# One core, attention and MLP block: last 64 rows of Q, K, V in halves of the array, a ninth key/value slot, residual in bf16, first two tiles side by side

## The chip, the cores and the metric

The kernel runs on one core of one Trainium2 chip. The metric is the device time of one execution in microseconds (us). TensorE is called PE here, VectorE DVE, ScalarE ACT, GpSimd POOL and the sync engine's DMA queue SP, as in the profile.

## The reference

`x` is 2048 rows of D = 576. There are 32 heads of 18, each position attends to 8 keys at distances 0, 2, ..., 14, and the MLP is F = 4608 wide.

```python
h  = x + attn(layernorm(x)) @ wo            # q, k, v = layernorm(x) @ wqkv
y  = layernorm(layernorm(h))
h2 = h + gelu(y @ w1 + b1) @ w2 + b2
```

Inputs and output are bf16.

## The kernel before

**Tiles.** Row 16p + j of `x` lies on partition p of tile j, so a tile has 128 rows and there are 16 tiles (n is the place in the order of work, j = `ORDER[n]`: the even tiles from 14 down, then the odd ones). A key at distance 2w is in tile j - 2w of the same partition, or, past the tile's start, in the partition above. Each parity has a window of eight slots (`kwin[e]`, `vwin[e]`). When a slot's tile has been used at its own place, it is wanted by the later tiles shifted by one partition: the kernel writes K and V of the tile to DRAM (`kvd`, task `bw`) and reads them back one row lower into the same slot (`ks`, `vs`), after that tile's product with the window is done.

**Stages per tile.** LayerNorm 1: statistics on DVE (`ln1a`), the root on POOL (`ln1r`), the normalising on DVE for the first eight tiles and on ACT for the rest (`ln1b`). The tile is padded with zeros from 576 to 640 columns and turned into `xnT`, by five PE transposes and an ACT copy for n < 8 (`t1`, `t1e`), by DMA for the rest. K, V and Q are each ten products 128x288 on PE (`chunk`, task `c`: two column halves of five blocks of 128 rows, the last block half zeros), evicted by ACT (`e`). Attention is on DVE: `p1a` (window times q), a tree of additions, `p1b` (maximum over the slots, subtract), exp on ACT, `p2n` (sum and divide), `p2a` (window times weights), additions to `o` (`p2b`). Then `o` is transposed (`t2`), by PE for n < 3 and by DMA after that, multiplied with `wo` (18 products, pairs of 64-row halves of the array), copied to `h` in f32 by ACT (`woe`), and DVE adds `x` and takes the statistics of LayerNorm 2 (`ln2a`); `hb` is `h` + b2 in bf16 for the end; `ln2b` normalises on ACT and `t3` transposes.

**MLP.** Two tiles make a group (eight groups). First come nine units `u`, 36 products each, in 64-row halves of the array, each followed by a gelu on ACT into `hT`. Then come four passes (two tiles times two column halves), each of 36 products 128x288 in nine pieces `m`, which add up in one PSUM bank `po`. After each pass DVE adds `hb` and writes `osb` (`fin`, task `out`), and after two passes the tile is stored. `po` is a pool of two tiles of one bank each; the other PSUM user is a pool `pm` of three tiles of two banks.

**Order.** All tasks are put in order while the kernel is built: `Weaver.run` takes, again and again, the task that can start first by costs written beside it, ties by priority, and records its instructions at once. Every engine then runs its instructions in that order. Waits between engines are put in by the tile framework from which instruction, in the order of recording, last wrote or read a tile.

Of the kernel before, what the change touches and what calls it, by code (L numbers as in the profile page):

```python
# [15 lines left out]
class Weaver:  # L16
# [4 lines left out]
    def __init__(self, slots):  # L21
        self.tasks = {}
        self.slots = {tag: [0.0] * n for tag, n in slots.items()}
        self.held = {}

    def add(self, name, engine, cost, fn, after=(), prio=0.0, take=None, give=(), lag=0.1, table=None, kb=0.0,
            backlog=2.5, transfers=1):
        assert name not in self.tasks, name
        self.tasks[name] = (engine, cost, fn, tuple(after), prio, take, tuple(give), lag, table,
                            (kb, backlog, transfers))  # L30


    RATE, TABLE, LANES = 240.0, 1.28, 8

    def run(self):
# [8 lines left out]
        table, queue, landed = None, 0.0, [0.0] * self.LANES  # L44
        while left:
            best = None
            for n in ready:
                engine, cost, fn, after, prio, take, give, lag, tab, (kb, backlog, transfers) = left[n]
                start = max([clock.get(engine, 0.0)] + [done[a][2 if done[a][0] == engine else 1] for a in after])
                if take is not None:  # L50
                    tag, key = take
                    if key not in self.held:
                        if not self.slots[tag]:
                            continue
                        start = max(start, min(self.slots[tag]))
                if kb:
                    start = max(start, queue - backlog, landed[transfers - self.LANES - 1])
                rank = (round(start, 3), prio, n)
                if best is None or rank < best:
                    best = rank  # L60
            assert best is not None, sorted(left)[:40]
            start, _, n = best
            engine, cost, fn, after, prio, take, give, lag, tab, (kb, backlog, transfers) = left.pop(n)
            ready.discard(n)
            if take is not None and take[1] not in self.held:
                tag, key = take
                free = min(self.slots[tag])
                self.slots[tag].remove(free)
                self.held[key] = tag
            fn()  # L70
            if tab is not None and tab != table:
                cost += self.TABLE
                table = tab
# [8 lines left out]
            for key in give:  # L82
                self.slots[self.held.pop(key)].append(done[n][1])
# [7 lines left out]
def kernel(  # L91
# [37 lines left out]
    dram = ctx.enter_context(tc.tile_pool(name="dram", bufs=1, space=bass.MemoryType.DRAM))  # L129
    ps_po = ctx.enter_context(tc.tile_pool(name="ps_po", bufs=2, space=bass.MemoryType.PSUM))  # L130
    ps_pm = ctx.enter_context(tc.tile_pool(name="ps_pm", bufs=3, space=bass.MemoryType.PSUM))

    kvd = dram.tile([NT, P + 1, 2 * D], BF16, name="kvd")
# [15 lines left out]
    kwin = [wpool.tile([P, W, D], BF16, name=f"kwin{e}") for e in range(2)]  # L149
    vwin = [wpool.tile([P, W, D], BF16, name=f"vwin{e}") for e in range(2)]  # L150
# [16 lines left out]
    HB, HT, LG, NQ = 4, 9, 4, 13  # L167
# [3 lines left out]
    wv = Weaver({"po": 2, "pm": 3, "oT": 1, "h": 2, "xr": 2, "hb": HB,  # L171
# [5 lines left out]


    TP, TO = 8, 3
    SLACK = 0.6  # L180
    WARM = 11
# [9 lines left out]
    def x_load(n):  # L191
        def fn():
            nc.sync.dma_start(out=T["x", n][:, 0:D], in_=x3[:, ORDER[n], :])
# [9 lines left out]
    def wq_rest(eng, t):  # L203
        return lambda: eng.dma_start(out=wqkv_sb[0:64, 4, t * D:(t + 1) * D], in_=A_wqkv[512:576, t * D:(t + 1) * D])
# [30 lines left out]
    Q, K, V = 0, 1, 2  # L235
    for n in range(NT):
        if n < LENT:
            T["x", n] = kwin[1][:].rearrange("p w c -> p (w c)")[:, n * DP:(n + 1) * DP]
        elif n < LENT + XH:
            T["x", n] = hn_bufs[0][:].rearrange("p a b -> p (a b)")[:, (n - LENT) * DP:(n - LENT + 1) * DP]  # L240
        else:
            T["x", n] = early.tile([P, DP], BF16, name=f"x{n}")[:]
        load(f"x{n}", x_load(n), 147, prio=0.1 * n if n else -300)
    for t in (K, V, Q):
        eng, at = (nc.scalar, -200) if t == K else (nc.sync, 0.55 if t == Q else 0.75)
        for r, (part, fn, kb) in enumerate((("a", wq_load(eng, t, 0, 2), 295), ("b", wq_load(eng, t, 2, 4), 295),
                                            ("c", wq_rest(eng, t), 74))):
            add(f"W{t}{part}", "ACT" if t == K else "SP", 0.5, fn, (), at + 0.01 * r, lag=1.8, kb=kb)

    def b2_load():  # L250
        nc.sync.dma_start(out=b2_bc[:], in_=B_b2.partition_broadcast(P))
        nc.sync.dma_start(out=kvd[:, 0, :], in_=w2_sb[0:NT, 0:2, :].rearrange("p a c -> p (a c)"))

    load("b2", b2_load, 150, prio=8.5, issue=0.7, transfers=2)
# [6 lines left out]
    for c in range(W1C):  # L261
        for half in range(2):
            for k in range(0, KC, W1K):
                bulk(f"w1{c}{half}{k}", w1_chunk(c, half, k), 295, prio=20 + c)
    for c in range(W2C):
        bulk(f"w2{c}", w2_chunk(c), 295, prio=30 + c, after=("b2", "b1t", "warm"))
# [5 lines left out]

    for n in range(NT):
        nc.vector.memset(T["x", n][:, D:DP], 0.0)
        if n in (1, 3, 5):
            t = (K, V, Q)[n // 2]
            nc.vector.memset(wqkv_sb[64:128, KT - 1, t * D:(t + 1) * D], 0.0)
    nc.vector.memset(w2_sb[0:NT, 0:2, :], 0.0)


    def warm():
        pw = ps_pm.tile([P, 1024], F32, tag="pm", name="warm")
# [3 lines left out]
    add("warm", "PE", 5.0, warm, (), -400, take=("pm", "warm"), give=("warm",))  # L286

    def b1_turn():
        T["b1T"] = ps_pm.tile([P, 2048], BF16, tag="pm", name="b1T")[:, 0:FT]
# [26 lines left out]
    def transposed(src, shifted=False):  # L316
        starts = [kt * P for kt in range(KT)] + ([64 + kt * P for kt in range(KT - 1)] if shifted else [])
        pt = ps_pm.tile([P, 2048], BF16, tag="pm", name="pt")[:, 0:len(starts) * P]
        pt = pt.rearrange("p (k t) -> p k t", t=P)
        for k, c0 in enumerate(starts):  # L320
            nc.tensor.transpose(pt[:, k, :], src[:, c0:c0 + P], ident[:])
        return pt

    def region(n):
        return n if n < LENT else (0, 1, 2, 3, 0, 1, 0)[n - LENT]


    def front(n):  # L330
# [3 lines left out]
        def ln1a():  # L334
            ln_stats(L1, n, T["x", n][:, 0:D])
            if n >= W:
                ln_var(nc.vector, L1, n, (1.0, EPS))

        def ln1r():
            if n < W:  # L340
# [6 lines left out]
        def ln1b():  # L347
            if n < W:
                nc.vector.tensor_scalar(out=T["x", n][:, 0:D], in0=T["x", n][:, 0:D], scalar1=L1["mv"][:, n, 0:1],
                                        scalar2=L1["rs"][:, n, :], op0=ALU.subtract, op1=ALU.mult)  # L350
            else:
                nc.scalar.activation(out=T["x", n][:, 0:D], in_=T["x", n][:, 0:D], func=ACT.Identity,
                                     scale=L1["rs"][:, n, :], bias=nmr[:, n, :])

        def t1():
            T["pt1", n] = transposed(T["x", n])

        def t1e(by_dma=False):
            if n < 2 * LENT:
                flat = (vwin if n < LENT else kwin)[1][:].rearrange("p w c -> p (w c)")  # L360
                r = region(n)
                T["xnT", n] = flat[:, r * DP:(r + 1) * DP].rearrange("p (k t) -> p k t", k=KT)
            else:
                T["xnT", n] = early.tile([P, KT, P], BF16, name=f"xnT{n}")[:]
            if by_dma:
                nc.sync.dma_start(out=T["xnT", n], in_=T["x", n], transpose=True)
            else:
                nc.scalar.copy(out=T["xnT", n], in_=T["pt1", n])  # L368

        add(f"ln1a{n}", "DVE", 1.07 if n < W else 1.2, ln1a, (f"x{n}",) + (("ln1b0",) if n == 1 else ()), prio=-20 + n if n < W else 0.5 + (n - W) // 4)  # L370
        add(f"ln1r{n}", "POOL", 0.95 if n < W else 1.1, ln1r, (f"ln1a{n}",), prio=-20, lag=0.1 if n < W else 1.0)
        add(f"ln1b{n}", "DVE" if n < W else "ACT", 0.45 if n < W else 0.7, ln1b, (f"ln1r{n}",), prio=-20 + n)
        freed = [m for m in range(LENT, n) if n < 2 * LENT and region(m) == region(n)][-1:]
        room = [f"t1e{m}" for m in range(LENT) if not freed and LENT <= n < 2 * LENT]
        room += [f"c{m}{c}" for m in freed for c in "QKV"]
        if n < TP:
            add(f"t1{n}", "PE", 0.45, t1, [f"ln1b{n}"] + room, prio=-60, take=("pm", f"t1{n}"), lag=0.3)
            add(f"t1e{n}", "ACT", 0.7, t1e, (f"t1{n}",), prio=-150, give=(f"t1{n}",))
        else:
            load(f"t1e{n}", lambda: t1e(True), 164, [f"ln1b{n}"] + room, prio=-20 + n, issue=1.2, lag=3.0)  # L380

        def chunk(t):
            def fn():
                pq = ps_pm.tile([P, 1024], F32, tag="pm", name="pq")
                T["pq", n, t] = pq
                for half in range(2):
                    c0 = t * D + half * HALF
                    p0 = 512 - HALF + half * HALF  # L390
                    for kt in range(KT):
                        nc.tensor.matmul(pq[:, p0:p0 + HALF], lhsT=T["xnT", n][:, kt, :],  # L392
                                         rhs=wqkv_sb[:, kt, c0:c0 + HALF],
                                         start=(kt == 0), stop=(kt == KT - 1))
            return fn

        def evict(t):
            def fn():
# [3 lines left out]
                else:  # L402
                    dst = (kwin if t == K else vwin)[e][:, s, :]
# [329 lines left out]
```

## Time and profile before

| | us |
|---|---|
| median of 3 runs (lowest, highest) | 382.62 (382.17, 382.90) |
| the profiled execution, whole | 382.82 |
| its span, first to last instruction | 381.0 |
| first PE instruction starts, last product's end | 1.17, 377.60 |
| PE busy, share of the span | 373.8, 98% |
| DVE busy, share | 292.5, 77% |
| ACT busy, share | 209.0, 55% |

The granted PE clock is 1.00 throughout. Products overlap, so the mean duration of one (286 ns for 128x288) is not its price: their starts lie 123 ns apart. DMA is busy for about the first 100 us (weights, `x` and the shifts) and lightly after that.

### The profile page before, as it was taken

To read this page: it belongs to the slowest core of one execution; us is meant where nothing else is said; L and a number is where in the kernel's file an instruction comes from. 1 tells how busy PE (TensorE), PEld (TensorE's weight loads), DVE (VectorE), ACT (ScalarE), POOL (GpSimd) and SP (SyncE) were. 2 spreads that over 40 slices of the span, in tenths; PEclk is the share of its full clock that TensorE was granted. 3 is DMA by queue.
4 is the path that set the end of the run, shared out by engine and by line. 5 is a ranking of instruction groups with operands and counts; after the bars stand their busy time and mean duration, and the time that the engine had idled before them with its cause. 6 is when DMAs were issued, how large, how long until landed. Compare 5 with 4: busy or idle time off the path is not lost.

```text
span 381.0 us, 10766 instructions
## 1 busy us (share of the span) xinstructions
PE 373.8 (98%) x4618; PEld 304.8 (80%) x4618; DVE 292.5 (77%) x563; ACT 209.0 (55%) x437; POOL 32.4 (9%) x55
## 2 busy tenths in 40 slices
PE   7999999999999999999999999999999999999996
PEld 3777787788788887887788778877887788778874
DVE  7999999899999999999999899998968932010000
ACT  2896665888255762575257526870685088106700
POOL 3670011000110110010001100110011011000000
PEclk9999999999999999999999999999999999999999
DMA  8798999986523212352232333222313331000000
GB/s 254 229 193 273 211 226 236 308 270 199 99 48 101 69 22 64 50 80 62 48 94 64 49 77 82 48 65 61 80 41 56 93 80 25 11 15 19 2 17 15
DMA packets 63967, 38.48 MB, mean 101 GB/s; under 512 B 39520, under 2 KB 63904, under 8 KB 63920
## 3 DMA queue, kind: packets, MB, share of 16 engines
q1 hardware_dynamic: 63296, 37.13, 41.4%
q8 instruction: 36, 0.59, 0.6%
q10 hardware_dynamic: 624, 0.66, 0.5%
q14 instruction: 11, 0.09, 0.1%
HBM read 22.28 MB, written 6.52 MB: 76 GB/s over the span
## 4 chain that ended last, share of the span: by engine, by line
PE 72%; DVE 14%; DMA 2%; issue 1%; POOL 0%; ACT 0%; DVEq 0%; ACTq 0%
PE po L667 35%; PE pm L630 33%; PE pw L564 4%; DVE prod L444 3%; DVE prod L450 2%; DVE prod L485 2%; DMA kwin<-kvd 2%; DVE prod L491 1%; DVE l_st L306 1%; DVE prod L495 1%; DVE h L577 1%; DVE half L437 0%; DVE half L438 0%; DVE hb L590 0%; DVE lg L457 0%
## 5 line engine op out<-in xcount | busy, mean ns | idle before, releaser
L641 ACT ACTIVATE hT<-pm,b_sb 128x256 bf16<-128x256 f32 x288 | 112.5, 477 | 88.6 <-PE pm L630 88.3
L630 PE MATMUL pm<-hnT,w_sb 64*128 64x256 bf16 x2592 | 144.7, 269 | 0.0
L667 PE MATMUL po<-w_sb,hT 128*128 128x288 bf16 x1152 | 142.9, 286 | 0.0
L630 PEld LDWEIGHTS <-w_sb 64*128 64x128 bf16 x2592 | 125.7, 94 | 17.1 <-issue 1.8
L667 PEld LDWEIGHTS <-hT 128*128 128x128 bf16 x1152 | 111.9, 98 | 29.9 <-issue 2.0
L686 DVE TENSOR_TENSOR osb<-po,hb 128x288 bf16<-128x288 f32 x32 | 14.2, 453 | 56.0 <-PE po L667 56.0
L314 POOL TENSOR_TENSOR l_rs<-l_ve,mhalf 128x1 f32<-128x1 f32 x32 | 27.0, 844 | 277.8 <-DVE l_ve L310 277.2
L450 DVE TENSOR_TENSOR prod<-prod 128x2304 bf16<-128x2304 bf16 (+1 forms) x64 | 44.1, 690 | 1.5
L444 DVE TENSOR_TENSOR prod<-kwin,q 128x4608 bf16<-128x4608 bf16 x16 | 40.9, 2555 | 1.3 <-DMA kwin<-kvd 0.9
L485 DVE TENSOR_TENSOR prod<-vwin,at 128x4608 bf16<-128x4608 bf16 x16 | 40.9, 2554 | 0.5 <-ACT vwin L405 0.2
L594 ACT ACTIVATE hn<-h,nmr,l_rs 128x576 bf16<-128x576 f32 (+1 forms) x32 | 19.2, 652 | 23.1 <-issue 13.3
L392 PE MATMUL pq<-wqkv_sb,vwin 128*128 128x288 bf16 x210 | 27.5, 286 | 1.4 <-ACT vwin L368 0.8
L392 PE MATMUL pq<-wqkv_sb,kwin 128*128 128x288 bf16 x210 | 27.1, 286 | 0.0
L392 PEld LDWEIGHTS <-vwin 128*128 128x128 bf16 x210 | 20.1, 98 | 6.9 <-ACT vwin L368 1.2
L392 PEld LDWEIGHTS <-kwin 128*128 128x128 bf16 x210 | 20.2, 98 | 5.4 <-issue 0.5
L491 DVE TENSOR_TENSOR prod<-prod 128x2304 bf16<-128x2304 bf16 x16 | 21.7, 1358 | 0.6
L564 PE MATMUL pw<-wo_sb,oT 64*128 64x288 bf16 x288 | 20.3, 283 | 0.0
L577 DVE TENSOR_TENSOR h<-h,xr 128x576 f32<-128x576 f32 x16 | 12.0, 753 | 10.4 <-ACT h L569 10.4
L569 ACT COPY h<-pw 128x576 f32<-128x576 f32 x16 | 10.5, 654 | 15.4 <-PE pw L564 15.4
L564 PEld LDWEIGHTS <-oT 64*128 64x128 bf16 x288 | 13.6, 94 | 4.3 <-issue 1.2
L405 ACT CAST vwin<-pq 128x576 bf16<-128x576 f32 x16 | 10.2, 641 | 6.9 <-PE pq L392 6.9
L405 ACT CAST kwin<-pq 128x576 bf16<-128x576 f32 x16 | 10.2, 639 | 6.3 <-PE pq L392 6.3
(63 smaller groups left out, 224.8 us busy)
## 6 DMA issues: line engine op xcount, KB each, us to landing
w_sb<-in_B_w_dram SPq DMA_DIRECT2D x36, 288.0 KB, 5.7
xr<-in_A_x_dram SPq DMA_DIRECT2D x16, 144.0 KB, 2.3
out_dram<-osb SPq DMA_DIRECT2D x16, 144.0 KB, 1.9
kvd<-kwin SPq DMA_DIRECT2D x14, 144.0 KB, 4.4
kvd<-vwin SPq DMA_DIRECT2D x14, 144.0 KB, 4.0
kwin<-kvd SPq DMA_DIRECT2D x14, 144.0 KB, 3.0
vwin<-kvd SPq DMA_DIRECT2D x14, 144.0 KB, 2.1
wqkv_sb<-in_A_wqkv_dram SPq DMA_DIRECT2D x4, 288.0 KB, 5.6
```

The source lines that it names most:

```text
L314: nc.gpsimd.tensor_tensor(out=L["rs"][:, n, :], in0=L["ve"][:, n, :], in1=mhalf[:], op=ALU.pow)
L392: nc.tensor.matmul(pq[:, p0:p0 + HALF], lhsT=T["xnT", n][:, kt, :], rhs=wqkv_sb[:, kt, c0:c0 + HALF], start=(kt == 0), stop=(kt == KT - 1))
L405: nc.scalar.copy(out=dst.rearrange("p (d h) -> p d h", h=H), in_=src.rearrange("p h d -> p d h"))
L444: nc.vector.tensor_tensor(out=prod[:], in0=kwin[e][:], in1=T["q", n][:].unsqueeze(1).to_broadcast([P, W, D]), op=ALU.mult)
L450: nc.vector.tensor_tensor(out=pv[:, :, 0:b - a, :], in0=pv[:, :, 0:b - a, :], in1=pv[:, :, a:b, :], op=ALU.add)
L485: nc.vector.tensor_tensor(out=prod[:].rearrange("p w (d h) -> p w d h", d=Dh, h=H), in0=vwin[e][:].rearrange("p w (d h) -> p w d h", d=Dh, ...
L491: nc.vector.tensor_tensor(out=prod[:, 0:4, :], in0=prod[:, 0:4, :], in1=prod[:, 4:8, :], op=ALU.add)
L564: nc.tensor.matmul(pw[:, half, 0:HALF], lhsT=T["oT", n][lo:lo + 64, block(c, half), :], rhs=wo_sb[lo:lo + 64, c, :], start=(c == 0), stop= ...
L594: nc.scalar.activation(out=hn_slots[n % 2][:, c0:c1], in_=src, func=ACT.Identity, scale=L2["rs"][:, n, :], bias=nmr[:, n, :])
L630: nc.tensor.matmul(pm[:, half, q, 0:width], lhsT=w1_sb[lo:lo + 64, c, f0:f0 + P], rhs=T["hnT", g][lo:lo + 64, block(c, half), 0:width], st ...
L641: nc.scalar.activation(out=T["hT", g, u][:, half, q, 0:width], in_=T["pm", g, u][:, half, q, 0:width], func=ACT.Gelu_apprx_tanh, bias=b1_s ...
L667: nc.tensor.matmul(T["po", n, half][:], lhsT=T["hT", g, u][:, r, q, a * P:(a + 1) * P], rhs=w2_sb[:, ft, half * HALF:(half + 1) * HALF], s ...
```

## The change

1. **Q, K, V.** The last 64 rows of the product are no longer padded. `xnT` and `wqkv_sb` hold these rows twice, on partitions 0 to 63 and 64 to 127; each column half takes its own copy in its own half of the array (`rest`). Eight 128-row products and one pair of 64-row ones take the place of ten. Two chunks that follow each other put their pairs back to back (`table="flip"`). The copies are made by two more 64-column transposes per PE transpose (`transposed`, 64 columns to one half of the PSUM partitions), by the loads `dup` for tiles turned by DMA, and by `wq_rest`. `xnT` now lies in the end of `w2_sb`, so the second half of the w2 chunks is loaded after the tiles' products.
2. **Window.** One tile of 17 slots for both parities; the shift is one SBUF to SBUF transfer of 127 partitions into the next slot, after the tile before. `p1a` and `p2a` skip one slot and are two instructions in most tiles. `kvd` and its transfers are gone.
3. **Softmax.** Three instructions over the slots become one `tensor_reduce`, for the maximum and for the sum.
4. **Residual.** `h` is bf16 and becomes `h` + b2 in place after `ln2b`; `hb` as a tile is gone.
5. **PSUM.** One pool of four tiles of two banks. Until Q, K and V are done the fourth serves transposes and products; from then on it is the tile `pos`, whose two banks are the two `po` of before.
6. **Start.** `x` of the second tile is loaded through the ACT queue at once, half of K's weights through SP; statistics of tile 1 go ahead of the normalising of tile 0, which is done in two pieces, as is its eviction; most clearing on DVE is gone, and one of eleven warming products.
7. The planner knows a price for changing between 64-row and 128-row work on PE, several costs are new, and the group units wait for all Q, K, V products.

```diff
-                for half in range(2):
-                    ...
-                    for kt in range(KT):
-                        nc.tensor.matmul(pq[:, p0:p0 + HALF], lhsT=T["xnT", n][:, kt, :], ...
+            blocks = [(half, kt, 0, P) for half in range(2) for kt in range(KT - 1)]
+            rest = [(half, KT - 1, 64 * half, 64 * half + 64) for half in range(2)]
+            todo = rest + blocks if wv.table["PE"] == "64" else blocks + rest
+            for half, kt, lo, hi in todo:
+                ...
+                nc.tensor.matmul(pq[:, p0:p0 + HALF], lhsT=T["xnT", n][lo:hi, kt, :],
+                                 rhs=wqkv_sb[lo:hi, kt, c0:c0 + HALF], ...
 ...
+    def transposed(key, src, tail, shifted=False):
+        ...
+        for k in range(KT - 1):
+            nc.tensor.transpose(pt[:, k, :], src[:, k * P:(k + 1) * P], ident[:])
+        for lo, c0 in ((0, D - 64), (64, tail)):
+            nc.tensor.transpose(pt[lo:lo + 64, KT - 1, :], src[:, c0:c0 + 64], ident[:])
 ...
-            load(f"ks{n}", lambda: nc.sync.dma_start(out=kwin[e][:, s, :], in_=kvd[n, 0:P, 0:D]),
+                return lambda: nc.sync.dma_start(out=win[1:P, b, :], in_=win[0:P - 1, a, :])
 ...
+            nc.vector.tensor_reduce(out=dst[:], in_=src[:].rearrange("p w h -> p h w"), axis=AX.X, op=op)
 ...
-            T["h", n] = sb.tile([P, D], F32, tag="h", name="h")
+            T["h", n] = sb.tile([P, D], BF16, tag="h", name="h", bufs=HB)
 ...
-                    if u == 0:
-                        T["po", n, half] = ps_po.tile([P, HALF], F32, tag="po", name="po")
+                    if u == 0:
+                        T["po", n, half] = T["pos"][:, wv.spot[f"po{n}.{half}"][1], 0:HALF]
 ...
+    def pos():
+        T["pos"] = banks("pos", [2, 512], F32)
+    add("pos", "-", 0.0, pos, qkv_done, take=("px", "pos"), lag=0.0)
```

## The prediction, written before the changed kernel ran

> **What bounds the kernel now.** First the page's busy shares, then PE's own waits.
>
> ```profile
> span 381.0 us, 10766 instructions
> PE 373.8 (98%) x4618; PEld 304.8 (80%) x4618; DVE 292.5 (77%) x563; ACT 209.0 (55%) x437; POOL 32.4 (9%) x55
> ```
>
> ```profile
> PE warm L284 <- DVE w_sb L269: 1.2, 1, 1.2
> PE pq L392 <- ACT vwin L368: 0.8, 1, 0.8
> PE pt L321 <- DVE kwin L349: 0.7, 2, 0.5
> PE pt L321 <- ACT hn L594: 0.6, 1, 0.6
> PE pq L392 <- ACT vwin L405: 0.6, 1, 0.6
> ```
>
> That is all PE ever waits for: under 4 us in 381, and nothing after 104 us. DVE, at 77%, ends its work before PE. So a microsecond of PE work added or removed, or of PE waiting, is a microsecond of the end. Then the timeline of PE, for the price of its work:
>
> ```profile
> 40.28 2.61 PE L392 MATMUL pq<-wqkv_sb,kwin 128*128 128x288 bf16 x20
> 42.82 1.27 PE L564 MATMUL pw<-wo_sb,oT 64*128 64x288 bf16 x18
> 44.03 8.75 PE L392 MATMUL pq<-wqkv_sb,kwin 128*128 128x288 bf16 x70
> ...
> 61.05 2.62 PE L392 MATMUL pq<-wqkv_sb,kwin 128*128 128x288 bf16 x20
> 63.51 2.61 PE L392 MATMUL pq<-wqkv_sb,xnT 128*128 128x288 bf16 x20
> ```
>
> Twenty products followed by more of their kind take 63.51 - 61.05 = 2.46 (123 ns each); followed by 64-row products they take 42.82 - 40.28 = 2.54. One by one, the starts lie 123 ns apart within a kind, 218 from 128-row to 64-row, 215 back (a 64-row pair itself 3 + 120). So **a change between the two costs 95 ns**, either way; the same excess stands between units and passes (201 for 106) and at the transposes (151 for 56). Last, the end of DVE's timeline, for a hand-over from PE:
>
> ```profile
> 368.82 0.46 DVE L686 TENSOR_TENSOR osb<-po,hb 128x288 bf16<-128x288 f32 x1 [3.95 <-PE po L667]
> 373.23 0.46 DVE L686 TENSOR_TENSOR osb<-po,hb 128x288 bf16<-128x288 f32 x1 [3.95 <-PE po L667]
> 377.64 0.46 DVE L686 TENSOR_TENSOR osb<-po,hb 128x288 bf16<-128x288 f32 x1 [3.95 <-PE po L667]
> ```
>
> DVE stands idle before each, so these starts show the hand-over bare: 377.64 is 0.32 after the start of the pass's last product (377.32). The passes lie 4.41 apart, 36 products of 123 ns: PE goes on through the evictions, because the next pass has a tile of its own.
>
> **PE's work.** The start apart (next part), 45 of the 48 Q, K, V chunks remain. Each loses two 128-row products and gains a pair: 2 x 122.5 - 123 = 122 ns, -5.5 us. The built order has 80 changes between 64-row and 128-row work where there were 28; 76 of them lie after the start, so 48 x 0.095 = +4.6. The halves thus pay for themselves with only 0.9 to spare. Fourteen transposes into two 64-column halves also leave the 128-column shape and come back: the trace has no such shape. Bounds: 0, if it is no change, and 95 ns each way, as every change that the trace has; I take 95, since all four kinds measured the same. Eleven sets after the start: 22 x 0.095 = +2.1 (0 to 2.1). The transposes themselves come to the same (80 and 14 pairs of about 56 ns for 94). Net +1.2.
>
> [...]
>
> **The start.** Before, the third K chunk ends at 13.06, or 12.78 without the transposes of the fourth tile, which now come later. After: tile 0 lands at 3.35 (landing records), and its statistics need no longer stand behind the clearing (3.77 before). Statistics, aggregate and variance 1.15, tile 1's statistics 0.98: the first normalising at 5.5, after the root (0.55 on POOL). Tile 2's statistics stand ahead of tile 1's normalising (6.9 to 7.25). PE, in order, then turns tile 1 to 7.8; K0 to 9.1; turns tile 2 to 9.7; K1 and K2 with three changes to 12.1. That is -0.7 (0 to -1.2; two of the column changes and one warming product less lie inside PE's waiting here).
>
> **Waits that go.** The hole at 27.9 (0.7, a PSUM tile not yet evicted) should go with the fourth PSUM tile; the one at 102.8 (0.75, LayerNorm 2 of the third tile) with DVE's shorter list: per tile the reductions save about 0.3 each (0.70 in three instructions before; one over 256 elements is nearest to the 0.43 of the 256-element subtract, with 0.19 and 0.75 as ends), the bf16 adds 0.35 each (0.75 against the 0.39 to 0.46 of bf16 work on 576 columns), and split products cost about 0.06 each. -1.5. If DVE's cover were gone, the holes would come back, +1.5.
>
> **Transfers.** The shifts no longer wait for their tile's own product; landing in 2.1 to 4.4 us as today's, they are ahead of DVE by a tile. On SP the DMA transpose of the ninth tile now stands behind all of wo, two shifts and eight w1 loads: 8.5 MB with everything before it, which at the 214 to 257 GB/s of the first 40 us is there at about 36, and PE wants it at about 40; at the slowest slice's 193 GB/s it would land at 40.6 (0 to +0.6, taken as 0). The last w2 chunks wait for the last products (about 75) and bring 1.5 MB, 7 us; the passes want them after 92. Both at nothing, hidden by PE's own work.
>
> So far: +1.2 - 0.7 - 1.5 = -1.0.
>
> **A wait that comes.** Both `po` are now one tile, `pos`. The built order shows what the tile framework makes of that. Before, the first product of a pass waits for the eviction two passes back. Now (last pass, its fifth product):
>
> ```
> 9198 L732 Matmult pm<-w_sb,hT 128x288
> 9199 L732 Ldweights hT
> 9200 L732 Matmult pm<-w_sb,hT 128x288 [waits DVE_49]
> ```
>
> The count it waits for is that of the eviction of the *pass just before*, in the other bank; and that eviction waits for the fourth product of this pass. In the order of recording, the eviction stands after the new pass's first piece and before its second, and the framework holds each to the other, though they touch different columns. So PE issues its piece, waits until DVE has evicted, and goes on. Queued behind the waiting product: all of PE. Price from the rows above: 0.32 (start of the product to DVE's start) + 0.46 (eviction) + 0.06 (end of a DVE instruction to PE, 6.14 to 6.20 at the first transpose) - 0.12 (the ordinary distance) = **0.72 us**. Of the 32 evictions, the fourth of a group is followed by units, which don't touch `pos`, and three third ones are placed behind the last pass. That leaves 21 where the waiting product is the very next: +15.1.
>
> In the last two groups (6 of the 21) DVE has nothing else, and 0.72 is firm. In the other 15 DVE may come late: before, its evictions start 0.3 to 5.6 us after the pass's last product. But now 8 to 24 products of the next pass are placed ahead of the eviction, so as to meet DVE, and every stall puts PE further behind its plan. I take 0.1 each, +1.5 (0 to 4.5, at 0.3 each).
>
> [...]
>
> **Sum.** -1.0 + 15.1 + 1.5 = +15.6. The tail after the last product (3.4 to the span's end, 1.8 outside the span) is unchanged. The profiled execution's 382.82 becomes 398.5; the median is 0.20 under that execution: **398.3**.
>
> **The rivals.**
>
> *The wait is hidden; the other sign.* If the eviction were done before PE gets to its waiting product, only the -1.0 stays: 381.6. It decides at one point: hand-over and eviction, 0.84, would have to fit in one product's 0.12, or other PE work would have to stand between. The order has none in those 21 places. About 0.2% (0.77 us) is what a measurement can tell from no change, so this case is split: faster 0.03, same 0.02.
>
> *Column halves are no change of mode.* -2.1: 396.2. For: both shapes use all 128 rows, and row halves are all that the trace has. Chance 0.15.
>
> *DVE comes late.* If DVE reaches each of the 15 evictions 0.6 later than its PE product allows, they cost 15 x 0.6 = 9.0 in place of 1.5: 405.8. For: DVE is dense up to 104 us, and a 2.6 us product may stand ahead. Against: placement, and DVE's 0.9 or more per tile saved. Chance 0.14.
>
> *The column halves are dear*, not side by side and not overlapped, at the 219 ns that one transpose lasts: 2 x 219 less the pair's 56 and one change of 95, about 0.28 more for each of 11 sets, 401.4. Chance 0.04.
>
> The forecast keeps 0.62. The range takes it with its bounds (396.7 to 401.3), and the free column halves without late DVE (394.6, nearly): 395.0 to 402.8. Faster 0.03, same 0.02, slower 0.95.
>
> **What would show it.** PE's waits would have a new first line, products on DVE's `osb`, some 21 times, about 0.6 to 0.7 each as idle time and 15 to 17 us in all; in the last group the evictions would lie about 5.1 us apart in place of 4.41. Starts 218 and 215 apart around the pairs show the changes' price, and the gap from the last full transpose to the first half shows the column mode's. I am wrong if PE's waits for DVE stay under 5 us, or if the passes of the last group still take 4.41.

## The result, and the profile after

| | us |
|---|---|
| changed kernel, median of 4 runs (lowest, highest) | 443.84 (443.18, 444.74) |
| kernel before, on the same chip | 382.76 (382.17, 382.91) |
| ratio, 95% interval | 1.160 (1.158 to 1.163) |
| the profiled execution, whole, its span | 443.57, 441.8 |
| start of the last PE product, before and after | 377.32, 438.15 |

The change costs 61 us. The forecast was 398.3, with 402.8 as the upper end: slower, as it said, but by four times as much. The page of the changed kernel, its first rows:

```profile
span 441.8 us, 10675 instructions
PE 391.9 (89%) x4631; PEld 302.1 (68%) x4631; DVE 279.3 (63%) x500; ACT 208.9 (47%) x435; POOL 36.9 (8%) x62
...
PE   6979567968994798989999999999999999999996
...
PEclk9898968997996899999999999999999999999999
DMA  6463946955546114851466573652531132100000
GB/s 210 127 158 78 191 115 60 197 125 177 179 144 43 45 42 73 63 83 45 65 60 77 75 59 45 55 72 44 79 70 43 27 83 40 30 13 16 1 14 14
```

PE falls from 98% to 89% of the span. Each digit is a fortieth of it, 11 us: most of the holes lie in the first fourteen, and there the granted clock falls too. In the first nine slices the DMA engines move 60 to 210 GB/s, where the kernel before moved 190 to 310, though there is less to move (34.6 MB for 38.5). PE's waits, the longest first:

```profile
PE pm L732 <- DVE osb L751: 17.8, 21, 6.4
PE pm L477 <- DMA w_sb<-hnT: 8.9, 1, 8.9
PE pm L371 <- ACT hn L660: 7.6, 2, 5.2
PE pm L631 <- DMA oT<-o: 4.2, 2, 2.6
PE pm L477 <- DMA wqkv_sb<-in_A_wqkv_dram: 2.4, 2, 1.9
PE pm L340 <- DMA w_sb<-in_B_b_dram: 1.9, 1, 1.9
```

The first line is the wait that was forecast, at 21 places. The others are not in the forecast: PE waits for transfers, or for ACT and DVE, which wait for transfers themselves. DVE's waits show it:

```profile
DVE h L644 <- DMA xr<-in_A_x_dram: 32.5, 3, 16.7
...
DVE l_st L356 <- DMA hnT<-in_A_x_dram: 7.9, 1, 7.9
```

The chain that ended last, in order of time (start, length, what), has loads of 8.7 to 16 us in its first 140 us; the longest transfer in the chain of before is one of 5.7:

```profile
1.66 9.63 DMA wqkv_sb<-in_A_wqkv_dram
...
35.73 16.06 DMA w_sb<-in_B_w_dram
...
61.20 8.71 DMA xr<-in_A_x_dram
...
82.18 13.38 DMA xr<-in_A_x_dram
...
123.80 12.50 DMA xr<-in_A_x_dram
```

`xr` is a plain load of 144 KB, unchanged by the diff. It is late because of what stands ahead of it.

**Why the loads are late: the landing records.** The trace has the times at which a transfer adds to its count as it lands. A load of before leaves 16 of these records close together (the first tile's: 2.87 to 3.35), as many as the page counts DMA engines, and I read them as one an engine. The first shift of the changed kernel is issued at 12.33 and leaves one record at 13.43 and one at 22.86, 10.5 us after the issue. (The records are times without counts: that the early one stands for the other 15 is worked out, 16 less the late one.) A load that comes behind such a shift has 15 records together and one straggler: a load of `w1` issued at 43.97, while a shift issued at 34.02 is still under way (its last record comes at 50.60), has 15 from 51.2 to 51.95 and the last at 56.46. So I read a shift of 127 partitions as lying on a single DMA engine, and a load behind it as late as its own sixteenth on that engine. There are 28 shifts. From its one early record to its late one the first takes 9.4 us; 15 of them, all issued after 136 us, where few loads stand beside them, take about 7.3, and the slowest, at 34 us, takes 14.5. The 28 times sum to 237 us, 222 without what overlaps; eight shifts are issued while another is under way and land 7.4 to 10.0 us after it, as if all lay on the same engine. The K shifts are issued from 12.3 to 266.4. The loads `wq_rest`, two times 64 rows with the doubling as the slowest dimension, are bound the same way, but by two engines: that for K is issued at 1.66, its early record comes at 2.88 and its two late ones at 10.32 and 11.28; a load of `wqkv` issued at 4.27 has 14 records from 7.63 to 8.78 and two stragglers, at 10.71 and 11.31.

**The last groups**, where DVE has nothing else to do, show the forecast wait bare. DVE's timeline (start, length, then the idle time before it):

```profile
385.95 0.46 DVE L751 TENSOR_TENSOR osb<-pm,h 128x288 bf16<-128x288 f32 x1 [7.76 <-PE pm L732]
391.06 0.46 DVE L751 TENSOR_TENSOR osb<-pm,h 128x288 bf16<-128x288 f32 x1 [4.66 <-PE pm L732]
396.18 0.46 DVE L751 TENSOR_TENSOR osb<-pm,h 128x288 bf16<-128x288 f32 x1 [4.66 <-PE pm L732]
```

The evictions lie 5.12 apart, 4.41 before. In the starts of the single products the gap at the fifth product is 0.835 in place of 0.122: 0.71 a place. And the column halves (PE's timeline):

```profile
48.91 0.39 PE L371 MATMUL pm<-ident,o 128*128 128x128 bf16 x4
49.22 0.25 PE L373 MATMUL pm<-ident,o 128*64 128x128 bf16 x2
49.40 0.40 PE L376 MATMUL pm<-ident,o 128*128 128x128 bf16 x4
```

The gap from the last full transpose to the first half is 149 ns, 56 within a kind: 93 ns for the change. The two halves start 3 to 4 ns apart, and the gap back to full transposes is 176, 120 more than 56.

### The profile page after: what moved, and what is told of

Its sections match the earlier page's. It is cut to its first block, busy times and chain, and to the rows that moved or that the text cites. A ratio compares the mean times of both kernels' runs of the same rounds, so it can differ in the third digit from the quotient of the medians.

```text
span 441.8 us, 10675 instructions
## 1 busy us (share of the span) xinstructions
PE 391.9 (89%) x4631; PEld 302.1 (68%) x4631; DVE 279.3 (63%) x500; ACT 208.9 (47%) x435; POOL 36.9 (8%) x62
## 4 chain that ended last, share of the span: by engine, by line
PE 64%; DMA 19%; DVE 9%; SPq 4%; ACT 2%; issue 1%; ACTq 0%; DVEq 0%
PE pm L695 30%; PE pm L732 28%; DMA xr<-in_A_x_dram 8%; DMA w_sb<-in_B_w_dram 4%; PE pm L631 3%; DVE prod L503 2%; DVE osb L751 2%; DMA oT<-o 2%; DMA wqkv_sb<-in_A_wqkv_dram 2%; DMA hnT<-in_A_x_dram 2%; SPq L428 2%; PE pm L477 2%; DVE l_st L356 2%; DVE prod L510 1%; ACT hn L660 1%
## 5 line engine op out<-in xcount | busy, mean ns | idle before, releaser
L732 PE MATMUL pm<-w_sb,hT 128*128 128x288 bf16 x1152 | 148.3, 288 | 17.8 <-DVE osb L751 17.8
L477 PE MATMUL pm<-wqkv_sb,w_sb 128*128 128x288 bf16 (+1 forms) x480 | 67.5, 309 | 11.7 <-DMA w_sb<-hnT 8.9
L477 PEld LDWEIGHTS <-w_sb 128*128 128x128 bf16 (+1 forms) x480 | 40.5, 102 | 36.2 <-issue 15.7
L751 DVE TENSOR_TENSOR osb<-pm,h 128x288 bf16<-128x288 f32 x32 | 14.4, 456 | 67.7 <-PE pm L732 67.7
L547 DVE TENSOR_TENSOR prod<-vwin,at 128x4032 bf16<-128x4032 bf16 (+7 forms) x30 | 41.8, 1432 | 0.3
L503 DVE TENSOR_TENSOR prod<-kwin,q 128x4032 bf16<-128x4032 bf16 (+7 forms) x30 | 41.7, 1429 | 0.1
L660 ACT ACTIVATE hn<-h,nmr,l_rs 128x576 bf16<-128x576 bf16 (+1 forms) x29 | 18.2, 675 | 28.0 <-DVE nmr L652 23.2
L631 PE MATMUL pm<-wo_sb,oT 64*128 64x288 bf16 x288 | 22.2, 295 | 4.6 <-DMA oT<-o 4.2
L636 ACT CAST h<-pm 128x576 bf16<-128x576 f32 x16 | 10.5, 655 | 27.4 <-PE pm L631 27.4
L452 ACT CAST kwin<-pm 128x576 bf16<-128x576 f32 x16 | 10.2, 638 | 21.0 <-PE pm L477 21.0
L656 DVE TENSOR_TENSOR h<-h,b_bc 128x576 bf16<-128x576 bf16 x16 | 7.3, 455 | 10.2 <-ACT hn L660 10.2
L356 DVE BATCH_NORM_STATS2 l_st<-h 128x6 f32<-128x288 bf16 x32 | 13.1, 452 | 0.6
L452 ACT CAST q<-pm 128x576 bf16<-128x576 f32 x16 | 10.2, 636 | 6.9 <-PE pm L477 6.9
```

Of the source, the lines that this page charges most:

```text
L356: nc.vector.bn_stats(out=st[:, c, :], in_=src[:, c * HALF:(c + 1) * HALF])
L477: nc.tensor.matmul(pq[:, p0:p0 + HALF], lhsT=T["xnT", n][lo:hi, kt, :], rhs=wqkv_sb[lo:hi, kt, c0:c0 + HALF], start=(seen[half] == 0), sto ...
L503: nc.vector.tensor_tensor(out=prod[:, at:at + hi - lo, :], in0=kwin[:, lo:hi, :], in1=T["q", n][:].unsqueeze(1).to_broadcast([P, hi - lo, ...
L547: nc.vector.tensor_tensor(out=prod[:, w0:w1, :].rearrange("p w (d h) -> p w d h", d=Dh, h=H), in0=vwin[:, lo:hi, :].rearrange("p w (d h) - ...
L631: nc.tensor.matmul(pw[:, half, 0:HALF], lhsT=T["oT", n][lo:lo + 64, block(c, half), :], rhs=wo_sb[lo:lo + 64, c, :], start=(c == 0), stop= ...
L660: nc.scalar.activation(out=hn_slots[n % 2][:, c0:c1], in_=src, func=ACT.Identity, scale=L2["rs"][:, n, :], bias=nmr[:, n, :])
```

## The experiments

Theory A: there are two losses, the late transfers by the few engines that their shapes are given, about 40 us, and the passes' wait, about 15. The rivals are named in each expectation.

**1 and 2. The shift in two parts; the rest rows in two loads; and both.** The edits:

```diff
-return lambda: nc.sync.dma_start(out=win[1:P, b, :], in_=win[0:P - 1, a, :])
+for p0, p1 in ((0, 112), (112, 127)):
+    nc.sync.dma_start(out=win[p0 + 1:p1 + 1, b, :], in_=win[p0:p1, a, :])
```

```diff
-src = bass.AP(..., ap=[[0, 2], [3 * D, 64], [1, D]])
-eng.dma_start(out=wqkv_sb[:, KT - 1, t * D:(t + 1) * D], in_=src)
+for lo in (0, 64):
+    eng.dma_start(out=wqkv_sb[lo:lo + 64, KT - 1, t * D:(t + 1) * D], in_=A_wqkv[D - 64:D, ...])
```

The shift alone:

> The changed kernel with each shift of a window slot as two transfers, of 112 and of 15 partitions, in place of one of 127; nothing else, and the same order of all other instructions. Theory A (few engines): in the changed kernel's trace a shift's completion comes as one update of 15 counts about 1 us after the issue and a single last one 5 to 30 us later, and every other transfer has 15 of its 16 landings together and one straggler; so each 127-partition shift sits on one of the sixteen DMA engines and everything behind it there is late. By A nearly all of the loss of the first 150 us, about 40 us, goes: 443.8 to 401 (398 to 408), what stays being the passes' waits (15 us) and some 3 us at the start from the last 64 rows of the weights. Theory B (order): the loss is the order on SP (transposes behind loads, w2 behind products), which is unchanged here: 440 to 447.

Measured 408.54 us (407.68 to 409.13), ratio 1.067 (1.065 to 1.069): 35.3 us back. That is 0.5 us above theory A's range (398 to 408), and far from theory B's. (In the trace of the changed kernel the two records of a shift lie 6.5 to 14.5 us apart, not 5 to 30, and loads with nothing slow ahead of them have their 16 together, as one issued at 50.62 has: 57.91 to 58.11.) The rest rows alone:

> The changed kernel with the last 64 rows of K's, V's and Q's weights loaded as two transfers of 64 partitions, in place of one whose outermost dimension is the two copies; the shifts stay as in the changed kernel. Theory A (few engines): the weights' share is small: K's rows land by about 7 in place of 11.3, PE saves 2 to 4 us at the start, and the later holes at the transposes and wo stay: 440 (436 to 444). Rival (the weights alone hold the queues up and all that follows is their echo): 405 to 420.

438.18 (437.26 to 439.62), ratio 1.145 (1.142 to 1.148): 5.7 us back, within theory A's range. Both:

> Both edits together: shifts in 112 and 15 partitions, last weight rows in two transfers of 64. Theory A: the first 105 us come back as forecast (PE's waits for DMA under 2 us, granted clock 1.00, the first unit starts at 73 to 75), and the 21 passes still wait 0.71 each: 382.8 - 1.0 + 15 to 16.5 = 396.5 to 399, sure within 394 to 403. Theory B (order on SP): 435 to 447.

404.60 (403.80 to 405.45), ratio 1.057 (1.055 to 1.059): 39.2 us of the 61 were transfers. PE's waits are then

```profile
PE pm L735 <- DVE osb L754: 14.0, 21, 3.0
PE pm L334 <- DVE w_sb L324: 1.2, 1, 1.2
PE pm L477 <- DMA w_sb<-hnT: 0.9, 1, 0.9
```

and among the longest three one is for a transfer, of 0.9. The expected 396.5 to 399 was missed by 6 us, and the wider 394 to 403 by 1.6: the order on SP (theory B) is out, but the change without its slow transfers costs more than the forecast had. Experiment 3 shows how much.

**3. Two separate output tiles as well.** The pool's fourth tile is closed where `pos` was made, and two tiles of one bank come in its place.

```diff
-T["pos"] = banks("pos", [2, 512], F32)
+psx_cm.__exit__(None, None, None)
+pso = ctx.enter_context(tc.tile_pool(name="pso", bufs=1, space=bass.MemoryType.PSUM))
+T["pos"] = lambda i: pso.tile([P, 512], F32, tag=f"po{i}", name="po")
```

> As the kernel with both transfer edits, and the two accumulators of the passes are again two PSUM tiles of one bank each, in the place of the fourth tile of two banks once Q, K and V are done. The instruction order of every engine is the same; only the waits differ: a pass's first product waits for the eviction two passes back. Theory of the passes' wait: 15 to 16 us less than with both transfer edits alone: 381.8 (380 to 384), no wait of PE for osb. Rival (the evictions' place in DVE's order holds the passes up anyway): 388 to 397.

386.65 (386.42 to 388.32), ratio 1.011 (1.009 to 1.013). The wait was worth 17.95 us. The two profiled executions are 17.1 apart, and the starts of their products, compared one by one, show where: 20 places of 0.71 make 14.2; at the twenty-first, at 146 us, PE stood 3.3 us, as DVE was late besides (3.2 more than the ordinary distance); behind that stall the granted clock was 0.50 for 3.4 us, and the products lost 1.8, nearly all of it there. Against that, this run has 2.1 us of stalls that the other lacks or has shorter.

The expected 381.8 (380 to 384) was missed by 4.9 us, although the gain was larger than expected, since the run before it already stood 6 us higher. The rival (388 to 397) is out. What is left in PE's waits, the longest (1.2, at the very start, as before) apart:

```profile
PE px L481 <- DMA w_sb<-hnT: 1.1, 1, 1.1
...
PE po L739 <- DVE osb L758: 0.8, 2, 0.6
PE pm L702 <- ACT hT L713: 0.7, 1, 0.7
```

**4. One row of 128 taken from the kernel before.** If the 127 rows are the cause, the kernel before must show it without any of the change.

```diff
-nc.sync.dma_start(out=kwin[e][:, s, :], in_=kvd[n, 0:P, 0:D])
+nc.sync.dma_start(out=kwin[e][1:P, s, :], in_=kvd[n, 1:P, 0:D])
```

and the same for `vwin`.

> The kernel before with one thing altered: its 28 shift reads out of DRAM fetch rows 1 to 127 instead of 0 to 127 (the slots' row 0 keeps what is there, so the output differs). Same route, same count, one row of 128 less. Theory A (a transfer of 127 rows lies on one of the 16 DMA engines, and all later transfers queue behind it there): far slower than 382.6, 410 to 440 us, by what the shifts cost in the changed kernel (39 us between it and the run with shifts and rest loads split); every read's completion comes as one count and a late last one. Theory B (the SBUF to SBUF route, or waiting on the shift before, is what is slow in the changed kernel): 382 to 384 us.

445.77 us (443.85 to 449.01), ratio 1.165 (1.162 to 1.167). Reading 127 rows in place of 128, 28 times, costs 63 us. (Row 0 is masked in the softmax, so the output stays the same, other than written above.) DVE's waits name the shifts themselves:

```profile
DVE prod L485 <- DMA vwin<-kvd: 27.0, 7, 6.5
DVE prod L444 <- DMA kwin<-kvd: 26.9, 8, 7.1
DVE h L577 <- DMA xr<-in_A_x_dram: 14.6, 2, 8.9
```

Theory A stands, and the SBUF to SBUF route is not needed for the loss. (The size was above the expected 410 to 440.) This edit also moves the first row from partition 0 to 1; that this is not the cause is seen in experiments 1 and 9, where parts of 112 and 126 rows are written from partition 1 on and leave 16 and 14 records together.

**5. One output tile in the kernel before.** The two `po` become the halves of one tile, nothing else:

```diff
-T["po", n, half] = ps_po.tile([P, HALF], F32, tag="po", name="po")
+if "pos" not in T:
+    T["pos"] = ps_po.tile([P, 2, 512], F32, tag="po", name="po")
+T["po", n, half] = T["pos"][:, half, 0:HALF]
```

> The kernel before with the two output tiles of the passes made the two halves of one tile, as the changed kernel has them; nothing else altered, DVE and the transfers as before. Theory A (a pass waits for the eviction of the pass just ahead of it, 0.712 us at 21 places): 382.5 + 15.0 = 397.5, within 396 to 400. Theory B (the wait stands in the shade of other work in this kernel, or is specific to the changed kernel's layout): under 390.

397.42 (397.19 to 398.00), ratio 1.039 (1.037 to 1.041): +14.8 for the expected +15.0. PE's waits and the last evictions of DVE:

```profile
PE po L669 <- DVE osb L688: 11.9, 21, 1.0
```

```profile
377.53 0.46 DVE L688 TENSOR_TENSOR osb<-po,hb 128x288 bf16<-128x288 f32 x1 [22.34 <-PE po L669]
382.65 0.46 DVE L688 TENSOR_TENSOR osb<-po,hb 128x288 bf16<-128x288 f32 x1 [4.66 <-PE po L669]
387.77 0.46 DVE L688 TENSOR_TENSOR osb<-po,hb 128x288 bf16<-128x288 f32 x1 [4.66 <-PE po L669]
```

21 places again and the same 5.12 apart. The view counts 11.9 us of idle time, 0.57 a place, since it takes a product as busy until its modelled end; the starts give 0.71.

**6. Two output tiles with the transfers left as changed.**

> The changed kernel with only the two output tiles of the passes as separate tiles; shifts and rest loads stay as changed. Theory A (the passes' wait and the late transfers are two separate losses): 443.8 - 21 x 0.71 = 428.9, with the 2 to 3 us that the longest wait holds 426 to 429. Theory B (in the first groups the wait stands in the shade of DVE, which is late by the transfers): 431 to 436, as only the places of the later groups give their 0.71 back.

431.25 (430.26 to 431.29), ratio 1.127 (1.124 to 1.129): 12.6 us back, which lies in theory B's range, at its lower end, and outside A's. Of the 18 that the wait costs with the transfers repaired, 5 stand in the shade of late transfers as long as these are there. In this run PE's stalls over 0.3 us before 160 us sum to 42.0 (40.3 in the changed kernel): what the passes gain in the early groups, a later transfer takes back (PE waits 11.3 us for one `oT` at 134). So the two losses don't simply add up: the transfers cost 39.2 us with the passes' wait in place and 44.6 (431.25 - 386.65) without it.

**7. The halves against full products.** Experiment 3 with the last 64 rows on all 128 again:

```diff
-rest = [(half, KT - 1, 64 * half, 64 * half + 64) for half in range(2)]
+rest = [(half, KT - 1, 0, P) for half in range(2)]
```

> The run with shifts and rest loads split and two output tiles (386.65 us), with the last 64 rows' products on all 128 rows again: per product group two full products in place of two halves side by side, no switch of form inside the group; instructions, order and transfers are the same (the last 64 rows are added twice, so the output differs). Theory A (a pair of halves saves 122 ns and its switch costs 95): slower by 48 x 0.027 = 1.3, less the switches at the borders, so 0.5 to 1.5 us slower: 387.2 to 388.2. Theory B (the switch is free where weights load ahead): 5.5 us slower, 392. Theory C (switches dearer than in the sum): faster than 386.6.

388.52 (386.88 to 389.84), ratio 1.015 (1.013 to 1.018) beside 1.011 (1.009 to 1.013) of experiment 3 in an earlier comparison: the intervals overlap, so the time alone decides nothing against A, but 5.5 us (B) is out. The starts of the products say it more sharply. In this profiled execution products and transposes from 6.8 to 13.9 us stood about twice as far apart as in experiment 3 (240 ns for 123), and by then it was 2.9 us behind; as that begins ahead of the first product that the edit touches, it is no effect of the edit. From the 61st product on neither execution has such a stretch; 45 of the 48 chunks lie there, and the gaps that are at most 0.3 us in both sum to 0.74 us more with full products. That is the halves' gain, where the forecast had 0.9 to spare.

**8. The DMA transposes earlier, and the warming product back.** `AHEAD` 8 for 5, then also `WARM` 11 for 10.

> The run with shifts and rest loads split and two output tiles (386.65 us), with AHEAD 8 in place of 5: the first DMA transposes are queued on SP ahead of the w1 loads. Theory A (what is left against 382.6 is PE's wait of 1.4 us at 41 and 0.7 at 53 us for the ninth tile's transpose and what follows it): 384.6, 384 to 385.5. Theory B (the start or DVE's lateness sets it): within 0.5 us of 386.65, or slower where the w1 loads come late for the first unit.

386.47 (386.20 to 387.59), ratio 1.011 (1.009 to 1.013): the wait of 1.4 at 41 us is gone, and the time is as expected by theory B, within 0.5 of experiment 3. Theory A fell. In the profiled execution the place of the wait is taken by slow products: the granted clock was 0.50 for 3.4 us from 8.6 on, which cost 1.5 us against experiment 3, where it was 1.00. That alone doesn't explain the median: the three executions with a mean granted clock of 1.0 took 386.20 to 386.47, only 0.2 less than the three of experiment 3 (386.42 to 386.68). What holds these up is not known, as none of them was profiled.

> The run with AHEAD 8 (386.47 us; single times from 386.2 at a granted clock of 1.0 to 387.6 at 0.996), with eleven warm-up products as in the kernel before instead of ten, so that TensorE's hole ahead of the first transposes is shorter by 0.43 us. Theory A (the hole at the start lets the clock fall to half for some us in part of the executions): every execution at clock 1.0, 386.0 to 386.6, spread under 0.6. Theory B (the spread has another cause): 386.2 to 387.6 as before. In both the remaining 3.7 us against 382.6 stay: 1.5 of more TensorE work (transposes in column halves) and 2.3 of waits on a late DVE at 117, 146, 174 and 190 us.

387.39 (387.02 to 388.05), ratio 1.014 (1.012 to 1.015). All four executions had a granted clock under 1.0, so theory A fell here too. Eight products from 8.5 to 12 us were 240 ns apart all the same, though the hole ahead of the transposes had shrunk to 0.84 from 1.03. It is a weak test: the hole shrank by 0.19, not by 0.43, and the second one of 1.04 us, behind the first tile's transposes, stayed.

**9. Other splits of the shift.** Experiment 3 with `((0, 96), (96, 127))`, then with `((0, 126), (126, 127))`.

> The run with shifts and rest loads split and two output tiles (386.65 us), with each shift in parts of 96 and 31 rows instead of 112 and 15. Theory A (a part is spread over the largest count up to 16 that divides its rows: 16 engines for 96, one for 31): the 31 rows lie on one engine, 31/127 of the changed kernel's load there (some 2.6 us a shift, by 10.5 us for 127 rows): 388 to 393 us. Theory B (only that 127 rows are not split evenly, or the count of transfers): 386 to 387.

> As the run before, in parts of 126 rows and 1. Theory A (126 divides by 14, so 14 engines take 9 rows each): 386 to 388 us, the shift landing within 1 us of the 112-row one. Theory B (rows must be a multiple of 16, else one engine): 430 to 433 us, as with two output tiles alone.

388.39 (387.14 to 389.33), ratio 1.016 (1.013 to 1.019), and 387.80 (386.61 to 388.49), ratio 1.014 (1.012 to 1.016). The landing records of the first shift, read as one an engine:

| rows | records together, the early one not counted | from the first record to the last |
|---|---|---|
| 127 | 1 | 13.43 to 22.86 |
| 126 | 14 | 11.77 to 13.66 |
| 112 | 16, no early one | 12.46 to 13.03 |
| 96 | 16, no early one | 13.23 to 13.42 |
| 31 | 1 | 13.01 to 16.45 |
| 15 | 15 | 12.15 to 13.20 |

That is the largest divisor of the rows up to 16 in each of the six cases, and rules out "a multiple of 16, else one engine". The 31 rows do lie on one engine, but cost no time that this comparison can tell from the split into 126 and 1, although 388.39 is within the 388 to 393 that was expected of them: the last product of the profiled execution starts 1.5 us later than with 126 and 1, and 1.3 of that are products 240 ns apart before 11.5 us. The 28 parts of 31 rows make 93 us of one engine's time, from the early record to the late one, and fit beside its share of the other loads, where the 237 of the 127-row shifts did not. The loss is not in proportion to the rows. That it sets in when the one engine is full is likely, but two sizes don't show it.

No run was faster than the kernel before, and none of them points to a version that would be.

## Why the prediction was wrong

**The step that failed is "Transfers".** It put the shifts as "landing in 2.1 to 4.4 us as today's" and "ahead of DVE by a tile", with no term in the sum, and the other late loads "at nothing". The first shift landed after 10.5 us, and the transfers cost 39.2 us (experiments 1 and 2; 44.6 without the passes' wait, experiment 6). The time of before belonged to shifts of 128 rows. The text took it over to 127 as if the price went by bytes, and counted bandwidth over all engines (8.5 MB at 214 to 257 GB/s) without asking how many engines a shape is given. The trace of before has no transfer of an odd number of rows, so a bound from both sides was due there, and for the shifts the step had none above. The doubled load of the rest rows was not costed at all: 5.7 us alone, 3.9 on top of the shift.

The late loads cost more than their waits. The changed kernel has the order of experiment 3, so their products can be compared one by one: of the 57 us between the two profiled executions, 11.6 are products that stand further apart, all of them in seven stretches of 3.4 to 10.2 us in which the granted clock was 0.50. (It was 1.00 throughout before, and up to the last product only one such stretch is left with both transfer edits.) The rest, 45.4, are longer stalls, the passes' wait included. Behind the long holes (9.1 us at 49.6, 5.5 at 95.5, 6.7 at 131.8) products stood 240 ns apart in place of 123, but there are stretches behind shorter holes too (2.2 us at 9.1 and at 30.1, then a granted clock of 0.50 from 12.8 and 33.3). What brings one on is not shown.

**Right, term by term:**

- *A wait that comes*: 0.71 measured for 0.72, at 21 places, alone in the kernel before +14.8 for +15.1. The forecast's "5.1 apart" is 5.12. The rival of a hidden wait is out.
- *DVE late*, +1.5 (0 to 4.5): 3.0, what experiment 3 gave back beyond 21 x 0.71. The size is in the range by luck: it was to be 0.1 at each of 15 places, and with the transfers repaired it was nothing at all but one, 2.5 us at 146, with a stretch of slow products behind it. That also speaks against the rival *DVE comes late*, which had 0.6 at each.
- *PE's work*, +1.2: the sum of the gaps up to 0.3 us rose from 367.25 to 368.75, +1.5. The column halves cost 93 ns a change on the way in for the 95 taken, 120 on the way back, so that they "are no change of mode" is out, and as they are side by side, they aren't as dear as that rival had them. A pair in place of two full products and the change that it brings nearly cancel, as forecast: 0.74 us in favour of the halves for 0.9 (experiment 7).
- *The start*, -0.7: with the loads repaired the third K chunk's last product starts at 12.21, 12.94 before. In the changed kernel it started at 15.66, held up by the K rest rows.

**Wrong in a smaller way:** *Waits that go*, -1.5. The holes at 27.9 and 102.8 are gone, but with everything repaired (experiment 3) there are new ones: 1.4 at 41, for the ninth tile's DMA transpose, which *Transfers* had at 0 to 0.6; 0.7 at 53; and 2.8 together at 117, 146, 174 and 190 us, where passes wait for DVE's evictions, and units for a DMA transpose and for ACT. So experiment 3 ends 4.0 above the kernel before (386.65 for 382.64): 1.5 of PE work, 2.4 of stalls over those of before. The sum had said 1.0 below. What brings these about is not settled. DVE had stood idle for loads of `x` (2.0 us between 8 and 25) and for `xr` (3.6 at about 50), but no run shows what they would be without that, and experiment 8, which took the wait at 41 away, didn't get the time back.

The whole, each step measured by its own run, in this order of repair: 382.6 + 4.0 (the change with its transfers and output tiles repaired) + 18.0 (the passes' wait) + 39.2 (transfers) = 443.8. Of the 45.5 us between forecast and result, the transfers are thus 39.2, the change itself 5.0 (4.0 for -1.0), and the wait with DVE's lateness 1.4 (18.0 for 16.6), within rounding.

## What to carry to other kernels

A shift of 127 rows in place of 128, 28 times, cost the kernel before 63 us, for fewer bytes. So don't price a transfer by its bytes alone: count its landing records, and cut a shift by one partition into parts that leave many together (112 and 15 rows left 16 and 15 here, and gave 35.3 us back). A slow transfer shows first as other loads being late, so when an unchanged load stands in the chain of waits, look at its landing records for one straggler, and then at what lies ahead on that engine. And two buffers that are meant to overlap must be two tiles to the framework: two halves of one tile cost a full hand-over, 0.71 us here, at each change.

## What the runs showed of the hardware

- A transfer of one row of 1152 bytes (experiment 9) left 16 landing records. Read as one an engine, it was spread over 16 engines along its 576 columns, the only dimension of more than one element.
- With little else beside it, one engine takes about 7.3 us for 127 rows of 1152 bytes inside SBUF (changed kernel, after 136 us) and 2.4 to 2.8 for 31 (experiment 9, after 100 us): by my estimate from these two, about 50 ns a row and 1 us in all beside that. In the first 100 us, beside other loads, the same shifts took 7.7 to 14.5.
- In the profiled executions of experiment 8 (both runs) and of 96 and 31 rows, the granted clock was 0.50 for 3.4 us from 8.1 to 8.6 us on, and in those of experiment 3 and of 126 and 1 rows it was 1.00. In experiment 7 products stood 240 ns apart up to 13.9 us, and yet the view of the stretch from 6 to 14 us gives a granted clock of 1.00: the view does not show every slow stretch. What brings such a stretch on at the start, no run here settles.
